# A short convolution's taps loaded in another way, beside newly chosen loads and schedule constants, in a fused convolution and gated-MLP kernel

## The chip, the cores and the metric

The kernel runs on one core of a Trainium2 chip. Its time is the device time of one execution in microseconds (us), and the median of several runs is what is compared. One further execution was recorded by the hardware profiler; its page and its trace are quoted below. The engines are PE (TensorE; PEld is its weight load), DVE (VectorE), ACT (ScalarE), POOL (GpSimd) and SP (SyncE, which here only issues DMA transfers). ACTq and SPq in a row are an engine's own queue issuing a DMA.

## The reference

The input x is 2048 x 640 in bf16. It is normalized, and the sum of x, a long convolution block (A) and a gated MLP (B) is returned.

```
xn = layernorm(x)
# A: a causal convolution of 4 taps over k, times v, then a convolution as long as the sequence
k_shift = sum over t of k_pad[:, t:t+S, :] * shift_k[:, 3-t]
kv = k_shift * v
y  = irfft(rfft(pad(kv)) * rfft(pad(ssm_k)))[:S] + kv * ssm_D
A  = xn * y
# B
h  = sigmoid(xn @ w_gate) * (xn @ w_up)        # 640 -> 1728
B  = h @ w_down                                # 1728 -> 640
return x + A + B
```

shift_k has the shape 640 x 4: for one channel its four taps lie side by side in memory.

## The kernel before

Rows of the sequence lie 16 to a partition (row 16 p + b in partition p), and the 640 channels are worked in five chunks c of 128. The MLP goes in four turns t of 512 rows. Within a turn, `gate(fc)` and `up(fc)` are each five matmuls of 128x512 for a block fc of 128 hidden columns (L246, L258). ScalarE puts the sigmoid of the gate into sig (L249), VectorE multiplies it with the up product into hT (L264). In some blocks ScalarE first casts the up product from PSUM (L261), and VectorE multiplies in place (L262). `both` does the last 64 columns, and `down` (L285) the product with wd, in two halves of seven matmuls for each 128 rows and 320 columns. The layernorm of a turn's rows is a chain on VectorE with the root on GpSimd (`ln_stats`, `ln_rstd`, `ln_nmr`, `ln_xn`), and `xn_tr` turns the result by TensorE into xnT (L217, copied at L220 or L222).

The long convolution is a Fourier transform in two stages for kv and for ssm_k side by side. `h_tr` turns ssm_k (tile hn) by TensorE into kvh (pht, L303). `kv_op` makes the four-tap convolution on VectorE: 16 operations of 128x1024 per chunk (L318 to L327), which read kx and the taps sc, laid out as tap by channel and the same in every partition. `st1` is the first stage (ps, L345), written to DRAM by `wr1` and read back in another order by `rd2` (tile t). `st2` (L373), `prod` (DVE) and `inv1` (L403) follow, then `wr2` and `rdb` go through DRAM again (tile bi), and `inv2` (psb, L435) ends a quarter of a chunk.

The taps are brought in through DRAM. At the start ScalarE's queue issues `tapT.rearrange("m d -> d m") <- A_shift_k` (L445), which turns 640 x 4 into 4 x 640, in single elements of two bytes. `load_taps(c)` (L143, on SyncE's queue) then reads four rows of 128 of it, broadcast to all partitions, into one of two buffers sc.

The start is written out by hand: four loads of x, the turned taps, weights in column blocks of 256 (`load_w`: a gate load and an up load each), then taps, kx and v of chunk 0 on SyncE, and dcl (ssm_D) and hn of chunk 0 on ScalarE's queue. TensorE runs 15 idle matmuls, then transposes of four row blocks with three idle matmuls between, then the first two blocks fc in half products of 256 columns (`half`, L236). `add_D` (POOL, L296) adds ssm_D to hn, and `h_tr(0)` follows.

All that follows is put in order when the program is built, by a planner that is itself in the kernel. It keeps for every engine when it is free and for every result when it is ready, by costs in the code, and emits the step that it holds to be ready. Each engine then works through its instructions in that order and waits where the plan was too early. A DMA costs the planner 0.45 on SP, at least 1.4 to start, its duration, and 1.6 until its data count as landed. DUE, slack, TURN and TH steer which chain comes first: DUE the step from which layernorm goes ahead of the tap products on VectorE, slack how far ahead of time a group of loads may be issued, TURN how the two ends of the convolution chain alternate on TensorE, and TH from which backlog of VectorE an up product is cast by ScalarE first. The transfers share eight completion semaphores in turn, so that an issue waits until the transfer eight before it has landed.

Of the kernel before, what the change touches and what calls it, by code (L numbers as in the profile page):

```python
# [10 lines left out]
BF16 = mybir.dt.bfloat16  # L11
F32 = mybir.dt.float32
U16 = mybir.dt.uint16
ACT = mybir.ActivationFunctionType
# [3 lines left out]
DM = 640  # L18
FF = 1728
P = 128  # L20
NB = S // P
NC = DM // P
NFC = 14
# [11 lines left out]
def _tables():  # L35

    p = np.arange(P)  # L40
    k1 = p + 0.25
    s1 = np.zeros((P, NB, 2, P))
    for b in range(NB):
        psi = 2 * np.pi * k1[None, :] * (16 * p + b)[:, None] / 2048.0
        s1[:, b, 0, :] = np.cos(psi)
        s1[:, b, 1, :] = -np.sin(psi)
    tb = s1.transpose(3, 2, 1, 0) / 2048.0
    th = 2 * np.pi * np.outer(np.arange(NB), np.arange(NB)) / 16.0
    c, s = np.cos(th), np.sin(th)
    s2 = np.block([[c, -s], [s, c]])  # L50
    a1 = np.block([[c.T, s.T], [-c.T, -s.T]])
    a2 = np.block([[-s.T, c.T], [-s.T, c.T]])
    small = np.stack([s2, a1, a2], 1)
    return _bf16_bits(s1), _bf16_bits(tb), _bf16_bits(np.concatenate([small] * NQ, 0))
# [3 lines left out]
def kernel(  # L58
# [14 lines left out]
    nc = tc.nc  # L73
# [6 lines left out]
    Dcol = A_ssm_D.rearrange("(d o) -> d o", o=1)  # L80

    s1bits, tbbits, smbits = _tables()
    S1d = nc.inline_tensor(s1bits, name="tabS1")
    TBd = nc.inline_tensor(tbbits, name="tabTB")
    SMd = nc.inline_tensor(smbits, name="tabSM")
# [2 lines left out]
    cv = ctx.enter_context(tc.tile_pool(name="cv", bufs=1))  # L88
    dr = ctx.enter_context(tc.tile_pool(name="dr", bufs=1, space=bass.MemoryType.DRAM))
# [30 lines left out]
    sync = nc.sync  # L120
    ctx.enter_context(tc.manual_schedule())

    tapT = dr.tile([4, DM], BF16, name="tapT")


    cin = [dict() for _ in range(NC)]

# [4 lines left out]
    def load_h(c, eng, n, lo, hi):  # L132
        d = cin[c]
        if n == 0:
            d["hn"] = cv.tile([P, S], BF16, name="hn")
            d["dcl"] = cv.tile([P, 1], BF16, name="dcl")
            eng.dma_start(d["dcl"][:, :], Dcol[c * P:(c + 1) * P, :])  # L137
        eng.dma_start(d["hn"][:, lo:hi], A_ssm_k[c * P:(c + 1) * P, lo:hi])

    def load_taps(c):  # L140
        sc = cv.tile([P, 4, P], BF16, name="sc", bufs=2)
        src = tapT.rearrange("(o m) d -> o m d", o=1)[:, :, c * P:(c + 1) * P]
        sync.dma_start(sc[:, :, :], src.to_broadcast((P, 4, P)))  # L143
        cin[c]["sc"] = sc

    def load_k(c, lo, hi):
# [13 lines left out]
    def load_w(eng, lo, hi):  # L160
        eng.dma_start(w[:, :, lo:hi], wgr[:, :, lo:hi])
        h = min(hi, 13 * P)
        eng.dma_start(w[:, :, UP + lo:UP + h], wur[:, :, lo:h])
        if hi == FF:
            eng.dma_start(w[:, :, FF:UP], wur[:, :, h:FF])
# [276 lines left out]

    for i in range(4):
        (sync, nc.scalar)[i % 2].dma_start(x[:, i, :], xr[:, i, :])
    nc.scalar.dma_start(tapT.rearrange("m d -> d m"), A_shift_k)  # L445
    load_w(sync, 0, 256)
    load_h(0, nc.scalar, 0, 0, S)
    load_w(sync, 256, 512)
    load_taps(0)
    load_halo(0)  # L450
    load_k(0, 0, NB)
    load_w(sync, 512, 768)
# [50 lines left out]
    def opsready(ops):  # L503
        made = set(m for o in ops for m in o[3])
        return max(when([t for t in o[2] if t not in made]) for o in ops)

    def emit(step):
        fn, args, ops = step
        ops = ops()
        fn(*args)  # L510
        for eng, dur, need, make in ops:
            at = when(need)
            if eng == "DMA":
                free["SP"] = max(free["SP"], at) + 0.45
                free["DMA"] = max(free["DMA"], free["SP"] + 1.4) + dur
                end = free["DMA"] + 1.6
            else:
                free[eng] = max(free[eng], at) + dur
                end = free[eng] + LAG[eng]
            for m in make:  # L520
                ready[m] = end
                if m[0] in count:
                    count[m[0]] += 1
# [12 lines left out]
    def prior(tag, *k):  # L536
        return (tag,) + k if min(k) >= 0 else None
# [77 lines left out]
    def s_load(fn, args, occ, need, make):  # L615
        return fn, args, lambda: [("DMA", occ, need, make)]

    chains = dict(sp=[], dve1=[], ln=[], kv=[], pool=[], inv=[], mid=[], front=[], out=[], sp_b=[], sp_k=[],
                  sp_v=[], sp_t=[], sp_h=[], bulk=[], sp_w1=[], sp_w2=[])
    for c in range(NC):  # L620
        if c:
            last = [prior("kvn", c - 2, 13)]
            chains["sp_t"].append(s_load(load_taps, (c,), 0.4, [prior("kvn", c - 2, 14)], [("taps", c)]))
            back = [("htr", c - 1, 1)] if c > 1 else []
            chains["sp_h"] += [s_load(load_h, (c, sync, 0, 0, 1024), 0.7, back, []),
                               s_load(load_h, (c, sync, 1, 1024, 2048), 0.7, back, [("hn", c)])]
            chains["sp_k"].append(s_load(load_halo, (c,), 0.3, last, [("hal", c)]))
            for i in range(4):
                chains["sp_k"].append(s_load(load_k, (c, 4 * i, 4 * i + 4), 0.7, last, [("k", c)] if i == 3 else []))
            for i in range(4):  # L630
                chains["sp_v"].append(s_load(load_v, (c, 4 * i, 4 * i + 4), 0.7, [prior("st1", c - 2, 7)],
                                             [("v", c)] if i == 3 else [("va", c)]))
            chains["pool"].append((add_D, (c,), lambda c=c: [("POOL", 0.35, [("hn", c)], [("D", c)])]))
        chains["front"] += [s_htr(c, 0), s_htr(c, 1)]
        chains["kv"] += [s_kv(c, [8 * h + n for n in ns]) for h in range(2)
                         for ns in ((0,), (1, 2), (3, 4), (5, 6), (7,))]
        chains["front"] += [s_st1(c, n) for n in range(8)]
        chains["sp_w1"] += [s_wr1(c, i) for i in range(4)]
        for s in range(4 * c, 4 * c + 4):
            chains["sp"].append(s_rd2(s))  # L640
            chains["mid"].append(s_st2(s))
            chains["dve1"] += [s_prod(s, 0), s_prod(s, 1)]
            if s % 2:
                chains["inv"].append(s_inv1(s // 2))
                chains["sp_w2"].append(s_load(wr2, (s // 2,), 2.4, [("ao", s // 2)], [("d2", s // 2)]))
        chains["sp_b"] += [s_rdb(c, n) for n in range(2)]
        chains["last"] = chains.get("last", []) + [s_inv2(c, m) for m in range(4)]
    def s_w(lo, hi):
        return load_w, (sync, lo, hi), lambda: [("DMA", (hi - lo) * 0.0095, [], [("w", f) for f in range(lo // P, NFC)])]

    def s_wd(lo, hi):
        return s_load(load_wd, (sync, lo, hi), 0.5 * (hi - lo), [], ["wd"] if hi == NFC else [])

    def s_x(g):
        return s_load(load_x, (sync, g), 1.8, [], [("x", g)])
# [2 lines left out]
    bulk.append((sync.dma_start, (SMt[:], SMd.ap()), lambda: [("DMA", 0.2, [], ["SM"])]))  # L658
    bulk.append(s_w(768, 1024))
    bulk.append((sync.dma_start, (S1t[:], S1d.ap()), lambda: [("DMA", 2.9, [], ["S1"])]))  # L660
    bulk += [s_w(1024, 1280), s_w(1280, FF), s_wd(0, 7), s_wd(7, NFC), s_x(1)] + chains["sp_v"][:4]
    bulk += chains["sp_h"][:2] + chains["sp_k"][:5]
    del chains["sp_k"][:5], chains["sp_v"][:4], chains["sp_h"][:2]
    chains["bulk2"] = bulk = [s_x(2), s_x(3)]
    bulk.append((sync.dma_start, (TBt[:], TBd.ap()), lambda: [("DMA", 2.9, [], ["TB"])]))
# [73 lines left out]
        emit(chains[k][pos[k]])  # L739
        pos[k] += 1  # L740

    DUE = (18, 20, 24)
    slack = dict(bulk=5.0, sp_k=3.0, sp_v=3.0, sp_h=2.0, bulk2=1.5)

    def side(now, at):

        again = True
        while again:
            again = False
            for k in ("sp_w1", "sp", "sp_w2", "sp_b", "sp_t", "bulk", "sp_k", "sp_v", "sp_h", "bulk2", "out"):  # L750
                h = head(k)
                if k in slack and free["DMA"] > now + slack[k]:
                    continue
                if h and free["SP"] < now + 0.5 and opsready(h[2]()) <= now + 0.1:
                    issue(k)
                    again = True
                    break
            for k in ("pool",):
                h = head(k)
                if h and free["POOL"] < now + 0.5 and opsready(h[2]()) <= now + 0.2:  # L760
                    issue(k)
                    again = True
            due = at >= DUE[min(pos["ln"] // 10, 2)]
            for k in ("dve1",) + (("ln", "kv") if due else ("kv", "ln")):
                h = head(k)
                if h and free["DVE"] < now + 1.2 and opsready(h[2]()) <= max(now, free["DVE"]) + 0.1:
                    issue(k)
                    again = True
                    break

    at, credit, TURN, TH = 0, 0, 2, 0.5
    while at < len(seq) or any(head(k) for k in chains):
        now = free["PE"]
        side(now, at)
# [55 lines left out]
```

## Time and profile before

| | before |
|---|---|
| median of 3 runs | 260.72 us (260.69 to 261.73) |
| the profiled execution | 261.89 us |
| its span | 260.1 us |
| TensorE busy | 244.8 us (94%) |
| VectorE busy | 182.3 us (70%) |
| ScalarE busy | 155.7 us (60%) |
| GpSimd busy | 9.0 us (3%) |
| moved by DMA | 54.85 MB |

A row of the timeline has the start, the duration, engine, line, operation, the tile written and the tile read, a count, and in brackets the idle time before it and what ended it. A row of the chain has the start, the length, and what the end of the kernel hung on in that time. A row of the stretches has, for a window in us, its length, the busy time of PE, PEld, DVE, ACT and POOL with their instruction counts, the granted TensorE clock, the share of the DMA engines in use, and GB/s. A row of the DMA issues ends with KB per transfer and the median us from issue to landing. A row of the groups has the shapes, a count, busy us and mean ns of one, and idle time before them.

### The profile page before, as it was taken

How to read it: one execution, taken by the hardware profiler on the slowest of the kernel's cores; microseconds unless marked ns; L12 is line 12 of the kernel's file. 1: busy time of each engine (PE TensorE's matmuls, PEld its weight loads, DVE VectorE, ACT ScalarE, POOL GpSimd, SP SyncE). 2: the span in 40 equal slices, each digit the busy share in tenths (PEclk: the TensorE clock that was granted, in tenths of full speed). 3: DMA queues.
4: the chain of work that ended last, by engine and by line, in shares of the span. 5: the costliest groups of instructions: out<-in, count | busy, mean ns of one | idle time of the engine just before them, and what ended most of it. 6: DMA issues, size and time to landing. Idle time of an engine off the chain costs nothing.

```text
span 260.1 us, 5955 instructions
## 1 busy us (share of the span) xinstructions
PE 244.8 (94%) x2469; PEld 143.7 (55%) x2469; DVE 182.3 (70%) x346; ACT 155.7 (60%) x198; POOL 9.0 (3%) x23
## 2 busy tenths in 40 slices
PE   8096899999999999999999999999999999999994
PEld 2054444557764545546786564555677554545773
DVE  4312069638799999999989998896617766873263
ACT  2141336653349788875587876998679667665000
POOL 4200000000100020010000000000000000000000
PEclk9659599999999999999999999999999999999999
DMA  7993799999999899985473999637569668481613
GB/s 169 48 76 90 173 231 357 336 349 304 255 255 335 214 323 318 262 228 174 130 203 131 245 321 334 206 107 229 179 211 257 152 179 216 147 285 47 192 48 122
DMA packets 92918, 54.85 MB, mean 211 GB/s; under 512 B 53532, under 2 KB 85980, under 8 KB 92636
## 3 DMA queue, kind: packets, MB, share of 16 engines
q1 hardware_dynamic: 89740, 53.62, 74.7%
q10 hardware_dynamic: 3152, 0.86, 3.0%
q8 instruction: 19, 0.31, 0.5%
q14 instruction: 7, 0.06, 0.1%
HBM read 36.12 MB, written 18.36 MB: 209 GB/s over the span
## 4 chain that ended last, share of the span: by engine, by line
PE 86%; DMA 10%; ACTq 3%; DVE 0%; issue 0%; POOL 0%; POOLq 0%
PE pd L285 24%; PE pu L258 21%; PE pg L246 20%; PE ps L345 7%; DMA hn<-in_A_ssm_k_dram 6%; PE psb L435 4%; PE psa L403 3%; PE ps L373 3%; ACTq L137 3%; DMA bi<-d 2%; PE pht L303 2%; PE pg L270 2%; PE pt L217 1%; DMA x<-in_A_q_dram 1%; DVE x L288 0%
## 5 line engine op out<-in xcount | busy, mean ns | idle before, releaser
L285 PE MATMUL pd<-wd,hT 128*128 128x320 bf16 x448 | 65.0, 299 | 0.0
L246 PE MATMUL pg<-xnT,w 128*128 128x512 bf16 x250 | 63.3, 385 | 0.0
L258 PE MATMUL pu<-xnT,w 128*128 128x512 bf16 x250 | 63.2, 384 | 0.0
L285 PEld LDWEIGHTS <-hT 128*128 128x128 bf16 x448 | 42.8, 98 | 17.5 <-issue 1.1
L249 ACT ACTIVATE sig<-pg 128x512 bf16<-128x512 f32 x52 | 31.5, 606 | 27.3 <-PE pg L246 23.9
L264 DVE TENSOR_TENSOR hT<-sig,pu 128x512 bf16<-128x512 bf16 x37 | 25.2, 681 | 28.3 <-PE pu L258 24.2
L376 ACT CAST xz<-ps 128x1024 bf16<-128x1024 f32 x40 | 38.5, 1018 | 9.0 <-PE ps L373 9.0
L348 ACT CAST t<-ps 128x1024 bf16<-128x1024 f32 x40 | 38.7, 1027 | 5.1 <-PE ps L345 4.0
L246 PEld LDWEIGHTS <-w 128*128 128x128 bf16 x250 | 23.9, 99 | 28.8 <-issue 2.4
L258 PEld LDWEIGHTS <-w 128*128 128x128 bf16 x250 | 23.8, 99 | 26.7 <-issue 2.7
L288 DVE TENSOR_TENSOR x<-pd,x 128x320 bf16<-128x320 f32 x32 | 15.5, 488 | 20.1 <-PE pd L285 19.8
L387 DVE TENSOR_TENSOR xz<-xz 128x2048 bf16<-128x2048 bf16 x20 | 24.5, 1224 | 0.6
L324 DVE TENSOR_TENSOR acc<-acc,tmp 128x1024 bf16<-128x1024 bf16 x30 | 20.8, 692 | 1.0
L345 PE MATMUL ps<-kvh,S1t 128*128 128x256 bf16 x160 | 20.9, 273 | 0.0
L322 DVE TENSOR_TENSOR tmp<-kx,sc 128x1024 bf16<-128x1024 bf16 x30 | 20.5, 685 | 0.2
L408 ACT CAST ao<-psa 128x1024 bf16<-128x1024 f32 x16 | 15.5, 1027 | 5.4 <-PE psa L403 5.4
L345 PEld LDWEIGHTS <-S1t 128*128 128x128 bf16 x160 | 15.6, 98 | 5.0
L186 DVE BATCH_NORM_STATS2 st<-x 128x6 f32<-128x320 bf16 x32 | 13.9, 477 | 2.6 <-DMA x<-in_A_q_dram 2.6
L304 ACT COPY kvh<-pht 128x1024 bf16<-128x1024 bf16 x10 | 9.7, 1036 | 9.8 <-PE pht L303 9.8
L439 DVE TENSOR_TENSOR yx<-psb,xn 128x512 bf16<-128x512 f32 x20 | 13.8, 689 | 1.3
L385 DVE STREAM_SHUFFLE xz<-xz 128x512 f32<-128x512 f32 x20 | 14.5, 727 | 0.1
L217 PE MATMUL pt<-ident,xn 128*128 128x128 bf16 x80 | 7.5, 237 | 6.5 <-ACT xn L203 6.5
(48 smaller groups left out, 173.2 us busy)
## 6 DMA issues: line engine op xcount, KB each, us to landing
d<-t SPq DMA_DIRECT2D x20, 512.0 KB, 4.7
t<-d SPq DMA_DIRECT2D x20, 512.0 KB, 5.4
d<-ao SPq DMA_DIRECT2D x8, 512.0 KB, 4.5
bi<-d SPq DMA_DIRECT2D x8, 512.0 KB, 5.3
kvh<-in_A_v_dram SPq DMA_DIRECT2D x16, 128.0 KB, 4.5
hn<-in_A_ssm_k_dram SPq DMA_DIRECT2D x8, 256.0 KB, 3.9
kx<-in_A_k_dram SPq DMA_DIRECT2D x16, 128.0 KB, 3.2
x<-in_A_q_dram SPq DMA_DIRECT2D x3, 640.0 KB, 6.2
```

The source lines that it names most:

```text
L246: nc.tensor.matmul(pg[:, :], lhsT=w[:, c, fc * P:(fc + 1) * P], rhs=xnT[:, c, :], start=(c == 0), stop=(c == NC - 1))
L249: nc.scalar.activation(sig[fc][:, :], pg[:, :], ACT.Sigmoid)
L258: nc.tensor.matmul(pu[:, :], lhsT=w[:, c, UP + fc * P:UP + (fc + 1) * P], rhs=xnT[:, c, :], start=(c == 0), stop=(c == NC - 1))
L264: nc.vector.tensor_tensor(hT[:, fc, :], sig[fc][:, :], pu[:, :], ALU.mult)
L285: nc.tensor.matmul(pd[:, :], lhsT=hT[:, fc, bb * P:(bb + 1) * P], rhs=wd[:, fc, es], start=(fc == 0), stop=(fc == NFC - 1))
L288: nc.vector.tensor_tensor(x[:, b, es], pd[:, :], x[:, b, es], ALU.add)
L322: nc.vector.tensor_tensor(d["tmp"][:, :, :], kx[:, lo + 3 - m:hi + 3 - m, :], sb(m), ALU.mult)
L324: nc.vector.tensor_tensor(d["acc"][:, :, :], d["acc"][:, :, :], d["tmp"][:, :, :], ALU.add)
L345: nc.tensor.matmul(ps[:, i, :], lhsT=S1[:, b, h, :], rhs=cin[c]["kvh"][:, b, :, :], start=True, stop=True)
L348: nc.scalar.copy(out=d["t1"][:, o:o + 4, :, :].rearrange("p b s c -> p b (s c)"), in_=ps[:, :, :])
L376: nc.scalar.copy(out=d["xz"][:, 0:2, 4 * n:4 * n + 4, :].rearrange("p s k c -> p k s c"), in_=ps[n].rearrange("p q e s c -> p (q e) s c"))
L387: nc.vector.tensor_tensor(xz[:, 1:3, :, :], xz[:, 0:1, :, :].to_broadcast((P, 2, 8, P)), xz[:, 1:3, :, :], ALU.mult)
```

## The change

The taps of a chunk, 128 x 4 numbers that lie together in memory, are now loaded as one run of 1 KB, the same for every partition (tile sraw), and an engine puts them into the order tap by channel (tile sc). GpSimd does so for chunk 0, ScalarE for the others. The turned copy in DRAM is gone. sc has one buffer in place of two, so the copy for a chunk follows the last tap product of the chunk before (`("kvn", c - 1, 14)`), and the load of sraw follows the copy of the chunk before. In the loads' order, the second row block of x (`s_x(1)`) goes ahead of the down weights, and chunk 1's hn and kx ahead of its v. The planner counts a DMA as landed after 1.2 in place of 1.6, and DUE, slack, TURN and TH have other values.

```diff
+    srow = A_shift_k.rearrange("d m -> (d m)").rearrange("(o n) -> o n", o=1)
...
-    tapT = dr.tile([4, DM], BF16, name="tapT")
...
     def load_taps(c):
-        sc = cv.tile([P, 4, P], BF16, name="sc", bufs=2)
-        src = tapT.rearrange("(o m) d -> o m d", o=1)[:, :, c * P:(c + 1) * P]
-        sync.dma_start(sc[:, :, :], src.to_broadcast((P, 4, P)))
+        cin[c]["sraw"] = cv.tile([P, 4 * P], BF16, name="sraw")
+        sync.dma_start(cin[c]["sraw"][:], srow[:, 4 * c * P:4 * (c + 1) * P].to_broadcast((P, 4 * P)))
+
+    def taps(c):
+        sc = cv.tile([P, 4, P], BF16, name="sc")
+        src = cin[c]["sraw"].rearrange("p (d m) -> p m d", m=4)
+        if c == 0:
+            nc.gpsimd.tensor_copy(sc[:, :, :], src)
+        else:
+            nc.scalar.copy(out=sc[:, :, :], in_=src)
         cin[c]["sc"] = sc
...
-    nc.scalar.dma_start(tapT.rearrange("m d -> d m"), A_shift_k)
     load_w(sync, 0, 256)
+    load_taps(0)
     load_h(0, nc.scalar, 0, 0, S)
     load_w(sync, 256, 512)
-    load_taps(0)
     load_halo(0)
...
-                end = free["DMA"] + 1.6
+                end = free["DMA"] + 1.2
...
-            chains["sp_t"].append(s_load(load_taps, (c,), 0.4, [prior("kvn", c - 2, 14)], [("taps", c)]))
+            chains["sp_t"].append(s_load(load_taps, (c,), 0.4, [("taps", c - 1)], [("sraw", c)]))
+            chains["act"].append((taps, (c,), lambda c=c: [("ACT", 0.6, [("sraw", c), ("kvn", c - 1, 14)],
+                                                            [("taps", c)])]))
...
-    bulk += [s_w(1024, 1280), s_w(1280, FF), s_wd(0, 7), s_wd(7, NFC), s_x(1)] + chains["sp_v"][:4]
-    bulk += chains["sp_h"][:2] + chains["sp_k"][:5]
+    bulk += [s_w(1024, 1280), s_w(1280, FF), s_x(1), s_wd(0, 7), s_wd(7, NFC)] + chains["sp_h"][:2]
+    bulk += chains["sp_k"][:5] + chains["sp_v"][:4]
...
-    DUE = (18, 20, 24)
-    slack = dict(bulk=5.0, sp_k=3.0, sp_v=3.0, sp_h=2.0, bulk2=1.5)
+    DUE = (8, 52, 56)
+    slack = dict(bulk=3.0, sp_k=3.0, sp_v=3.0, sp_h=1.5, bulk2=1.5)
...
-            for k in ("pool",):
+            for k, e in (("pool", "POOL"), ("act", "ACT")):
                 h = head(k)
-                if h and free["POOL"] < now + 0.5 and opsready(h[2]()) <= now + 0.2:
+                if h and free[e] < now + 0.5 and opsready(h[2]()) <= now + 0.2:
...
-    at, credit, TURN, TH = 0, 0, 2, 0.5
+    taps(0)
+    at, credit, TURN, TH = 0, 0, 4, 1.5
```

Since the order comes from the planner, the change moves rows on every engine. Three places follow. A row has the line, the operation, and the tile written and read with its shape.

The first is the start of ScalarE's program, its queue's DMAs among it. Before:

```order
L444 DMA x<-in_A_q_dram 128x640
L118 ACT_TABLE_LOAD
L118 ACTIVATE warm<-mhalf 128x4
L444 DMA x<-in_A_q_dram 128x640
L445 DMA tapT<-in_A_shift_k_dram 640x4x1
L137 DMA dcl<-in_A_ssm_D_dram 128x1
L138 DMA hn<-in_A_ssm_k_dram 128x2048
L203 ACTIVATE xn<-x,nmr,rstd 128x640 x2
```

With the change:

```order
L450 DMA x<-in_A_q_dram 128x640
L119 ACT_TABLE_LOAD
L119 ACTIVATE warm<-mhalf 128x4
L450 DMA x<-in_A_q_dram 128x640
L136 DMA dcl<-in_A_ssm_D_dram 128x1
L137 DMA hn<-in_A_ssm_k_dram 128x2048
L209 ACTIVATE xn<-x,nmr,rstd 128x640 x2
```

The turned load of 640x4 single elements is gone from between x and dcl; the rest is the same.

The second is SyncE's program behind its loads of x: weights, taps, kx and its three rows of overlap, and the third weight block. Before:

```order
L161 DMA w<-in_B_w_gate_dram 128x5x256
L163 DMA w<-in_B_w_up_dram 128x5x256
L161 DMA w<-in_B_w_gate_dram 128x5x256
L163 DMA w<-in_B_w_up_dram 128x5x256
L143 DMA sc<-tapT 128x4x128
L151 DMA kx_85<-in_A_k_dram 112x3x128
L152 DMA kx_85<-in_A_k_dram 15x3x128
L147 DMA kx_85<-in_A_k_dram 128x16x128
```

With the change:

```order
L167 DMA w<-in_B_w_gate_dram 128x5x256
L169 DMA w<-in_B_w_up_dram 128x5x256
L141 DMA sraw<-in_A_shift_k_dram 128x512
L167 DMA w<-in_B_w_gate_dram 128x5x256
L169 DMA w<-in_B_w_up_dram 128x5x256
L157 DMA kx_85<-in_A_k_dram 112x3x128
L158 DMA kx_85<-in_A_k_dram 15x3x128
L153 DMA kx_85<-in_A_k_dram 128x16x128
```

The load of the taps no longer follows the turned copy, and stands one weight block earlier.

The third is SyncE's program around the down weights wd; d is the write of the first Fourier stage, t the tile it comes from. Before:

```order
L165 DMA w<-in_B_w_up_dram 128x5x64
L169 DMA wd<-in_B_w_down_dram 128x7x640
L354 DMA d_396<-t_397 128x2048
L169 DMA wd<-in_B_w_down_dram 128x6x640
L171 DMA wd<-in_B_w_down_dram 64x640
L143 DMA sc<-tapT 128x4x128
L130 DMA x<-in_A_q_dram 128x2560
```

With the change:

```order
L171 DMA w<-in_B_w_up_dram 128x5x64
L129 DMA x<-in_A_q_dram 128x2560
L360 DMA d_391<-t_392 128x2048
L175 DMA wd<-in_B_w_down_dram 128x7x640
L141 DMA sraw<-in_A_shift_k_dram 128x512
L175 DMA wd<-in_B_w_down_dram 128x6x640
L177 DMA wd<-in_B_w_down_dram 64x640
```

Both down-weight loads now stand behind the first write d, and the load of chunk 2's taps, which follows ScalarE's copy of chunk 1's, stands between them. That copy comes on ScalarE behind the sigmoid of the tenth block fc of the first turn.

More of the change, by code (lines that the diff above doesn't have):

```diff
@@ L616, in s_load @@
         return fn, args, lambda: [("DMA", occ, need, make)]
-    chains = dict(sp=[], dve1=[], ln=[], kv=[], pool=[], inv=[], mid=[], front=[], out=[], sp_b=[], sp_k=[],
+    chains = dict(sp=[], dve1=[], ln=[], kv=[], pool=[], act=[], inv=[], mid=[], front=[], out=[], sp_b=[], sp_k=[],
                   sp_v=[], sp_t=[], sp_h=[], bulk=[], sp_w1=[], sp_w2=[])
```

## The prediction

> **What bounds the kernel now.** I read the table of busy time by stretch first, then the chain of work that ended last, then the timeline of the first 30 us. The stretches (columns: length, PE, PEld, DVE, ACT and POOL busy with instruction counts, granted clock, DMA share, GB/s):
>
> ```profile
> 3.00:6.00 3.00, 3.00 (x10) 1.04 (x9) 2.21 (x7) 0.00 (x0) 0.60 (x2) 1.00 1.07 254
> 6.00:9.00 3.00, 0.76 (x4) 0.14 (x2) 2.71 (x13) 0.00 (x0) 1.22 (x3) 1.00 1.47 62
> 9.00:12.00 3.00, 0.00 (x0) 0.00 (x0) 0.00 (x0) 0.00 (x0) 0.44 (x1) 0.50 1.51 48
> ...
> 15.00:18.00 3.00, 3.00 (x16) 1.86 (x15) 1.00 (x3) 0.48 (x1) 0.00 (x0) 0.50 1.02 77
> ...
> 30.00:40.00 10.00, 10.00 (x40) 4.12 (x39) 4.99 (x8) 3.44 (x7) 0.00 (x0) 0.85 1.00 236
> 40.00:60.00 20.00, 20.00 (x110) 10.64 (x109) 12.08 (x21) 12.22 (x18) 0.00 (x0) 1.00 1.08 345
> ...
> 80.00:100.00 20.00, 20.00 (x195) 10.07 (x193) 19.55 (x40) 17.09 (x22) 1.51 (x2) 1.00 1.00 294
> ...
> 220.00:240.00 20.00, 20.00 (x253) 10.15 (x252) 13.64 (x23) 13.10 (x19) 0.00 (x0) 1.00 0.52 161
> ```
>
> From 30 us to 240 us TensorE is busy all the time (first and last of the ten stretches of 20 us are shown; the lowest has 19.71). So nothing behind the start can be shortened except TensorE's own work, which the change leaves alone. The start is another matter: before 27 us the DMA engines are more than full (shares 1.51 and 1.02) while they move 48 to 77 GB/s, a third of what they move at the same share elsewhere. The chain and the timeline say who does that:
>
> ```profile
> 3.88 6.76 ACTq L137
> 10.68 16.04 DMA hn<-in_A_ssm_k_dram
> 27.10 1.93 PE pht L303 x16
> 29.03 2.13 PE pg L246 x5
> 31.16 2.00 PE pu L258 x5
> 33.17 1.08 PE pg L246 x5
> ```
>
> ```profile
> 12.24 0.92 ACT L203 ACTIVATE xn<-x,nmr,rstd 128x640 bf16<-128x640 bf16 x1 [9.58 <-issue]
> 18.95 1.39 PE L236 MATMUL pg<-xnT,w 128*128 128x256 bf16 x10 [0.33 <-DMA w<-in_B_w_up_dram]
> 20.46 3.11 PE L236 MATMUL pg<-xnT,w 128*128 128x256 bf16 x25
> 25.21 0.37 SPq L143 DMA_DIRECT2D sc<-tapT  x1
> ```
>
> ```profile
> hn<-in_A_ssm_k_dram ACTq DMA_DIRECT2D x1, 512.0 KB, 16.0
> kx<-in_A_k_dram SPq DMA_DIRECT2D x1, 512.0 KB, 6.0
> tapT<-in_A_shift_k_dram ACTq DMA_DIRECT2D x1, 5.0 KB, 23.5
> ```
>
> The turned load of the taps moves 5 KB in 2560 single elements and lands after 23.5 us. Three things hang on it. ScalarE's queue is stuck in the issue behind it (6.76 us at L137), so ScalarE normalizes nothing before 12.24. hn, on the same queue, takes 16.0 us where 512 KB of kx take 6.0, and TensorE's pht at 27.10 waits for it. And SyncE's queue stands at the load of sc until 25.21, with kx, the third weight block and v behind it.
>
> The Trainium skill ("DMA: Bandwidth & Descriptors", Queues, rings and completion order) says that each DMA engine takes turns, packet by packet, between the queues that have work for it. The trace agrees: SyncE's weights crawl beside ScalarE's elements.
>
> **The change, part by part.** Milestone: the first full gate matmul (third weight column block), at 29.03 now. What lies behind it is 260.1 - 29.03 = 231.1 us, of which the first two matmul groups ran at half clock, 2.13 + 2.00 against 2 x 1.08: 1.97 us too many.
>
> When does that milestone come in the changed kernel? The first statistics are not touched:
>
> ```profile
> 6.14 0.15 DVE L196 SCALAR_TENSOR_TENSOR nmr<-mv,rstd 128x1 f32<-128x1 f32 x1
> 7.44 0.15 DVE L196 SCALAR_TENSOR_TENSOR nmr<-mv,rstd 128x1 f32<-128x1 f32 x1
> 13.22 0.71 PE L217 MATMUL pt<-ident,xn 128*128 128x128 bf16 x5 [6.46 <-ACT xn L203]
> 20.18 0.44 PE L217 MATMUL pt<-ident,xn 128*128 128x128 bf16 x5
> 13.97 0.69 ACT L220 COPY xnT<-pt 128x640 bf16<-128x640 bf16 x1
> ```
>
> With its queue free, ScalarE can start xn at 6.3 and end at 7.2; the first transposes stand at 7.3 in place of 13.22. The second xn waits for its statistics (7.6) and ends at 8.5, the third follows after a 0.69 copy and ends at 10.1. TensorE goes 7.3 + 0.44, three idle matmuls, transposes from 8.6 to 9.05, three idle matmuls (0.65 at full clock, by the 1.08 of five), and starts the half gates at 9.7. The 40 matmuls of these halves cost 3.11 / 25 = 0.124 each, 5.0 us, and two more transposes 0.88: done at 15.6. The weights have to be there at 9.7 and 10.9: x, two blocks of 320 KB and hn are 1.82 MB, at the 254 GB/s of 3 to 6 us 7.2 us after 2: about 9.2. hn is there too, so pht runs at once, half of 1.93 at full clock. The milestone comes at **16.6**, and 29.03 - 16.6 = 12.4 us are gained, with the half-clock excess 14.4.
>
> This takes the clock as full. The trace shows the clock at 1.00 for 6 to 9 us and at half from 9 us, some 2.5 us after the idle matmuls ended at 6.76; now the pause is 0.6 us. If the clock is half all the same, the prologue goes at the old pace: 13.22 to 23.57 is 10.35 us, and pht 1.93, so the milestone would be 7.3 + 12.3 = 19.6, 3.0 us later.
>
> The Trainium skill ("TensorE: Matmul & The Clock Gate", Part 1: The HAM clock gate) puts both the fall after an idle window and the rise after sustained work at about 3.4 us. By it the clock stays up here, the same sum. The trace has a slower rise: cold from 27.10 to 33.
>
> **Copies.** Four 512-element copies on ScalarE and one on GpSimd are new. Nearest rows:
>
> ```profile
> L261 ACT CAST hT<-pu 128x512 bf16<-128x512 f32 x13 | 7.6, 587 | 4.3 <-PE pu L258 4.0
> L262 DVE TENSOR_TENSOR hT<-sig,hT 128x512 bf16<-128x512 bf16 x13 | 5.4, 418 | 2.7 <-ACT hT L261 2.5
> L264 DVE TENSOR_TENSOR hT<-sig,pu 128x512 bf16<-128x512 bf16 x37 | 25.2, 681 | 28.3 <-PE pu L258 24.2
> L115 POOL MEMSET wd<- 64x640 bf16 x1 | 0.6, 621 | 0.0
> ```
>
> ScalarE: 4 x 0.59 = 2.4 us on an engine that is busy 12.22 to 17.09 of 20 us in the rows above; at the same time 11 of the 13 casts of L261 disappear (6.5 us), whose products go back to VectorE at 681 in place of 418 ns: 2.9 us. Both lie beside TensorE's work and I cost them at nothing; VectorE's cover is thin at 80 to 100 us (19.55 of 20), and if it is gone they cost up to 2.9. The GpSimd copy has no row of its kind: no less than the 0.6 of a fill, say up to 2. It starts when hn and sraw are there (about 10) and its reader, the first VectorE product, also waits for kx, which is issued behind the first up weights (9.2, eight transfers before it) and takes 6.0: 15.2. So nothing, or up to 0.5.
>
> **Down weights.** The new SyncE order has sraw of chunk 2 between the two down-weight loads, and that load waits until ScalarE has read sraw of chunk 1, a copy that stands behind the tenth gate's sigmoid. From 16.6, fifteen groups of 1.08 and one pair of st1 groups (0.87) bring that gate to 33.7, its sigmoid to 34.3, the copy's end to 34.9, the issue of the second down-weight load to about 35.4 and of its tail to 36.1.
>
> ```profile
> 47.70 0.83 SPq L171 DMA_DIRECT2D wd<-in_B_w_down_dram  x1
> 58.57 1.90 PE pd L285 x14
> 60.48 0.87 PE ps L345 x8
> wd<-in_B_w_down_dram SPq DMA_DIRECT2D x1, 80.0 KB, 9.6
> ```
>
> With 9.6 us to landing they are there at 45.7. TensorE comes to the second half of the first down product, after 22 + 1 groups of 1.08, four pairs of st1 at 0.87 and one half of 0.95, at 16.6 + 24.8 + 3.5 + 0.95 = 45.9. Before, the margin was 59.5 - 57.3 = 2.2 us; now it is 0.2. I take 0.5 us of waiting, between 0 and 2.5.
>
> **Schedule constants.** The planner now counts on a landing 0.4 us earlier. Its sum for a read of t is 0.45 + 1.4 + 1.8 + 1.2 = 4.85 us, before 5.25.
>
> ```profile
> t<-d SPq DMA_DIRECT2D x20, 512.0 KB, 5.4
> bi<-d SPq DMA_DIRECT2D x8, 512.0 KB, 5.3
> PEld L435 <- DMA bi<-d: 0.8, 1, 0.8
> PEld L373 <- DMA t<-d: 0.4, 1, 0.4
> ```
>
> The trace has 5.4, so TensorE may stand up to 0.5 us at a read that is placed tight; now it waits 1.2 us for such reads in all. All 28 reads tight would be 28 x 0.4 = 11.2, but a wait also moves every later step away from its data. Between 0 (or 1.2 better, if the new order spares the old waits) and 11.2 I take 1.0, near the row of today.
>
> **The sum**, against the profiled execution (261.89 us, its span 260.1 plus 1.79 around it): 261.89 - 14.4 + 0.5 + 1.0 = 249.0. The median of the runs, 260.72, lies 1.17 below that execution, so the forecast is **247.8 us**.
>
> **Rivals.** (a) The loads become the bound of the first phase. Up to the first down product all weights (6.6 MB), x twice, hn, k, v, a table, three taps and two writes are 12.1 MB. At the 236 GB/s of 30 to 40 us this takes 2 + 51.3 = 53.3 us, 7.4 more than 45.9; at the 345 GB/s of 40 to 60 us 37, no wait. For it: kx and v in short rows, the slow mix. Against it: after the stall all of SyncE's work was issued anew from 25.21 on, and the 20 us behind show the faster pace with the same kinds of loads. It would give up to 255.2; chance 0.17, spread between.
>
> (b) The clock stays half in the prologue: 250.8; chance 0.08.
>
> (c) Slower: one buffer of taps. ScalarE's copy for the next chunk waits in ScalarE's order for VectorE's last tap product of this chunk, with sigmoids behind it, and TensorE has four accumulators before it stops. If VectorE, full from 80 us on, runs a half chunk late (eight products of 0.69, 5.5 us) at each of the four copies, 22 us are lost: 261.89 - 14.4 + 22 - 1.17 = 268. It decides from 3.6 us per copy, where the gain is used up. Against it: at 40 to 60 us VectorE is 12.08 of 20 busy, and the planner keeps the copy back until those products are due. Chance 0.04.
>
> (d) Nothing is freed: the tiny load of dcl, also two bytes a partition, stays on ScalarE's queue, and were it the blocker, all would remain: 260.7. But its later loads on SyncE's queue land in a median of 4.7 us:
>
> ```profile
> dcl<-in_A_ssm_D_dram SPq DMA_DIRECT2D x4, 0.2 KB, 4.7
> ```
>
> Chance 0.02.
>
> **How the numbers follow.** The forecast has 0.69. Low end: milestone at 15.6, no new wait and the old 1.2 gone gives 261.89 - 15.4 - 1.2 - 1.17 = 244.1; I take 244.3. High end: it takes in (b), the milestone with 2.5 for the down weights and 3 for tight reads (251.8), and most of (a): 255. Half a per cent, 1.3 us, is about what a measurement of this kernel can tell from no change. Faster by more than that: the forecast, (a) and (b), 0.94; within: (d) and a little of (c), 0.02; slower: the rest of (c), 0.04.
>
> **What would show it.** Right, if the first xn on ScalarE starts at 6.3, pht at about 15.6 and the clock is full from 6 us on; if hn lands within 8 us of its issue; if TensorE's idle time behind the milestone stays under 2 us. The down weights: a wait of TensorE for wd at about 46 us. (a) would show as waits for w between 20 and 40 us at DMA shares of 1. (c) would show as ScalarE idle before the copies with VectorE as what ended it. What would make the prediction wrong: many small waits for t and bi in the middle, from the shorter landing time.

## The result and the profile after

| | before | changed |
|---|---|---|
| median | 261.23 us (260.69 to 263.47, 4 runs) | 252.49 us (251.14 to 254.44, 4 runs) |
| the profiled execution, its span | 261.89, 260.1 us | 254.44, 252.3 us |
| TensorE busy | 244.8 us | 239.5 us |
| VectorE, ScalarE busy | 182.3, 155.7 us | 184.4, 152.3 us |

The ratio is 0.9656, its 95% interval 0.9567 to 0.9744: faster by 3.4%. The median before is 0.5 us above the one shown with the prediction, because a fourth run (263.47 us) has joined the three. The forecast was 247.8 us in a range of 244.3 to 255.0; the time lies 4.7 us above the forecast and inside the range. The profiled execution is the slowest of the four, so its waits are probably at the upper end.

The stretches of the changed kernel, with the columns of before (length; PE, PEld, DVE, ACT, POOL busy; granted clock, DMA share, GB/s):

```profile
3.00:6.00 3.00, 3.00 (x12) 1.00 (x10) 2.26 (x8) 0.00 (x0) 0.60 (x2) 1.00 0.82 243
6.00:9.00 3.00, 1.61 (x15) 0.88 (x15) 2.66 (x12) 2.38 (x4) 1.30 (x3) 1.00 0.72 222
9.00:12.00 3.00, 2.97 (x30) 2.30 (x29) 1.00 (x3) 1.55 (x3) 0.36 (x1) 1.00 1.04 320
12.00:15.00 3.00, 2.96 (x29) 2.44 (x28) 1.18 (x2) 1.16 (x2) 0.76 (x2) 1.00 0.98 178
15.00:18.00 3.00, 3.00 (x26) 1.82 (x25) 0.69 (x1) 2.46 (x4) 0.00 (x0) 1.00 0.95 252
...
30.00:40.00 10.00, 10.00 (x56) 5.29 (x55) 9.70 (x22) 7.67 (x11) 0.00 (x0) 1.00 1.06 341
40.00:60.00 20.00, 18.15 (x154) 12.62 (x153) 14.48 (x28) 6.88 (x10) 1.21 (x2) 1.00 0.97 283
...
100.00:120.00 20.00, 18.66 (x245) 11.99 (x244) 16.79 (x36) 13.42 (x17) 1.38 (x1) 1.00 1.02 285
120.00:140.00 20.00, 16.71 (x221) 9.90 (x220) 15.30 (x30) 12.18 (x16) 0.19 (x1) 1.00 0.54 155
```

Two things are to be seen. The start is mended: from 6 to 18 us the DMA engines move 178 to 320 GB/s where they moved 48 to 77, and the clock is full. But where TensorE had been busy for 20.00 of 20 us, it now stands for 1.85, 1.34 and 3.29 us in three stretches. Two of these before the change (the third, 40 to 60 us, stands in the prediction):

```profile
100.00:120.00 20.00, 20.00 (x236) 10.44 (x233) 19.20 (x42) 15.44 (x20) 1.20 (x2) 1.00 0.87 252
120.00:140.00 20.00, 20.00 (x320) 14.56 (x305) 18.50 (x34) 13.23 (x16) 0.00 (x0) 1.00 0.57 172
```

The timeline of the start, and the three large waits in the timeline of TensorE alone, all in the changed kernel:

```profile
6.25 0.92 ACT L209 ACTIVATE xn<-x,nmr,rstd 128x640 bf16<-128x640 bf16 x1 [3.59 <-DVE nmr L202]
9.64 0.71 PE L242 MATMUL pg<-xnT,w 128*128 128x256 bf16 x5
14.78 1.16 PE L309 MATMUL pht<-ident,hn 128*128 128x128 bf16 x16
15.78 1.24 PE L252 MATMUL pg<-xnT,w 128*128 128x512 bf16 x5
```

```profile
59.09 0.44 PE L379 MATMUL ps<-t,SMt 32*32 32x512 bf16 x16 [1.85 <-DMA t<-d]
108.80 0.31 PE L291 MATMUL pd<-wd,hT 128*128 128x320 bf16 x1 [1.25 <-DVE hT L280]
124.59 0.62 PE L441 MATMUL psb<-bi,TBt 128*128 128x128 bf16 x8 [2.73 <-DMA bi<-d]
```

The first xn starts at 6.25 (12.24 before). The milestone, the first full gate matmul, is at 15.94 in the chain of work; it was 29.03. That is 13.1 us, and with the 2.0 us of half clock 15.1 us are won. Some 7 us of it are given back later in this execution: from 16 to 240 us TensorE is busy 217.1 of 224 us.

### The profile page after: what moved, and what is told of

Read it like the earlier page. It is cut to its first block, busy times and chain, and to the rows that moved or that the text cites. A ratio compares the mean times of both kernels' runs of the same rounds, so it can differ in the third digit from the quotient of the medians.

```text
span 252.3 us, 5975 instructions
## 1 busy us (share of the span) xinstructions
PE 239.5 (95%) x2469; PEld 141.2 (56%) x2469; DVE 184.4 (73%) x346; ACT 152.3 (60%) x191; POOL 10.5 (4%) x24
## 4 chain that ended last, share of the span: by engine, by line
PE 75%; DMA 14%; ACT 5%; DVE 2%; issue 1%; SPq 1%; DVEq 0%
PE pg L252 20%; PE pu L264 19%; PE pd L291 16%; DMA bi<-d 8%; PE ps L351 6%; PE psb L441 4%; PE psa L409 3%; DMA d<-ao 3%; ACT xz L382 2%; PE ps L379 2%; DMA t<-d 2%; PE pg L242 2%; PE pht L309 1%; DMA x<-in_A_q_dram 1%; PE pt L223 1%
## 5 line engine op out<-in xcount | busy, mean ns | idle before, releaser
L291 PE MATMUL pd<-wd,hT 128*128 128x320 bf16 x448 | 65.0, 300 | 1.2 <-DVE hT L280 1.2
L252 PE MATMUL pg<-xnT,w 128*128 128x512 bf16 x250 | 62.2, 380 | 0.6 <-ACT xnT L226 0.6
L264 PE MATMUL pu<-xnT,w 128*128 128x512 bf16 x250 | 62.2, 380 | 0.0
L291 PEld LDWEIGHTS <-hT 128*128 128x128 bf16 x448 | 42.8, 98 | 19.3 <-DVE hT L280 1.6
L270 DVE TENSOR_TENSOR hT<-sig,pu 128x512 bf16<-128x512 bf16 x48 | 32.7, 681 | 25.3 <-PE pu L264 18.9
L382 ACT CAST xz<-ps 128x1024 bf16<-128x1024 f32 x40 | 38.6, 1022 | 16.6 <-PE ps L379 16.6
L226 ACT COPY xnT<-pt 128x640 bf16<-128x640 bf16 x14 | 9.6, 699 | 8.4 <-PE pt L223 8.2
L441 PEld LDWEIGHTS <-TBt 128*128 128x128 bf16 x160 | 9.5, 98 | 5.7 <-DMA bi<-d 3.7
```

The lines of the kernel that those rows point to most:

```text
L252: nc.tensor.matmul(pg[:, :], lhsT=w[:, c, fc * P:(fc + 1) * P], rhs=xnT[:, c, :], start=(c == 0), stop=(c == NC - 1))
L264: nc.tensor.matmul(pu[:, :], lhsT=w[:, c, UP + fc * P:UP + (fc + 1) * P], rhs=xnT[:, c, :], start=(c == 0), stop=(c == NC - 1))
L270: nc.vector.tensor_tensor(hT[:, fc, :], sig[fc][:, :], pu[:, :], ALU.mult)
L291: nc.tensor.matmul(pd[:, :], lhsT=hT[:, fc, bb * P:(bb + 1) * P], rhs=wd[:, fc, es], start=(fc == 0), stop=(fc == NFC - 1))
L382: nc.scalar.copy(out=d["xz"][:, 0:2, 4 * n:4 * n + 4, :].rearrange("p s k c -> p k s c"), in_=ps[n].rearrange("p q e s c -> p (q e) s c"))
L441: nc.tensor.matmul(ps[:, i, :], lhsT=TB[:, h, 4 * m + i, :], rhs=bi[:, h, 4 * (m % 2) + i, :], start=(h == 0), stop=(h == 1))
```

## The experiments

Each expectation was written before its run. Medians are from different sets of runs, so where a few us matter the ratio to the kernel before, with its 95% interval, is the safer number.

**The taps alone, the constants alone.** The first kernel is the changed one with all constants and the loads' order of before; the second is the kernel before with the new ones.

```diff
-                end = free["DMA"] + 1.2
+                end = free["DMA"] + 1.6
-    DUE = (8, 52, 56)
+    DUE = (18, 20, 24)
-    at, credit, TURN, TH = 0, 0, 4, 1.5
+    at, credit, TURN, TH = 0, 0, 2, 0.5
```

(slack and the order of the bulk loads likewise; the second kernel has the same lines the other way round.)

> The new way of the taps with the loads' order and all schedule constants of before. The profile of the changed kernel has its milestone (first full gate matmul) at 15.94 us, 13.1 earlier, and 2.0 less of half clock, but about 7 us of new waits of TensorE between 57 and 140 us. Theory P (the new constants place steps too early, and so make the waits): the waits go, 261.2 - 15.1 + 0.5 = 246.6 us, ratio to before 0.94. Theory R (the earlier start itself makes them: TensorE no longer trails the loads, and any order meets full DMA engines): waits of 6 us or more stay, 252 us or more, ratio 0.965 or more.

Measured: 252.75 us, ratio 0.9709 (0.9638 to 0.978). This is what R expected, but for another reason. The milestone is at 16.0 here too; only 2.8 us are lost in the middle. The rest is lost at the end, as VectorE's timeline of this kernel shows:

```profile
242.46 0.49 DVE L294 TENSOR_TENSOR x<-pd,x 128x320 bf16<-128x320 f32 x1 [1.41 <-PE pd L291]
243.57 0.69 DVE L445 TENSOR_TENSOR yx<-psb,xn 128x512 bf16<-128x512 f32 x1 [0.62 <-PE psb L441]
...
248.06 0.42 DVE L446 TENSOR_TENSOR x<-x,yx 128x512 bf16<-128x512 bf16 x1
```

The last down product is added at 242.9, and the last four products of the convolution follow alone until 248.5. In the order before, 42 down matmuls stood behind them; here none do. A new step in the planner (the copy) made another order, and this one puts the convolution last.

> The taps as before, through the turned copy, with the new order of loads and the new constants. Theory P: the new waits come in here too, 261 + 5 to 7 = 266 to 268 us. Theory R: the start is as late as before, so the new constants meet the same room as the old: 261 us, within 2.

Measured: 263.59 us, ratio 1.0107 (1.0039 to 1.0175). Between the two theories: the new constants cost under the late start, too, but 1% and not 2%.

**Single constants of the changed kernel.** In the first the landing time goes back to 1.6, in the second TURN and TH go back to 2 and 0.5, in the third the landing time is 2.0.

> The changed kernel with one constant back: a transfer counts as landed after 1.6 us in place of 1.2. If the landing time is what makes the waits (the part of P that the prediction priced at 1.0 us): 247 to 248 us and TensorE's waits for t and bi under 2 us in all. If not: 251 to 253 us.

Measured: 249.67 us, 0.9591 (0.9509 to 0.9672), the fastest of these, and TensorE's waits for bi are 2.4 us with none for t. It points to the landing time, but its interval and that of the change overlap.

> The changed kernel with TURN and TH of before (2 and 0.5). If the alternation or the fewer casts on ScalarE make the waits: 247 to 249 us. If they serve the earlier start (R): 252 us or more, with more casts at the line of the up product and ScalarE busier.

Measured: 257.47 us, 0.9872 (0.9808 to 0.9935), 5 us slower than the change. As in e1_taps_alone, the last products of the convolution come behind the last down product, on VectorE from 246.2 to 251.1 us. So in these kernels, with the copy in the plan, the new TURN and TH bring the convolution forward; with the old ones it ends last.

> The changed kernel with a landing time of 2.0 us in the planner (changed: 1.2, 252.5 us; 1.6: 249.7 us). If TensorE's waits come from steps placed ahead of their data, they shrink further and the time is 247 to 249 us. If the convolution chain, placed later, now ends behind the MLP, as with the old TURN and TH: 250 us or more, with an idle TensorE in the last 10 us.

Measured: 250.55 us, 0.9587 (0.9522 to 0.9652). Not further down than at 1.6: a later landing alone doesn't bring the waits to nothing.

**Does TensorE lack lead?** The changed kernel with a later TensorE:

```diff
-    busy(15)
+    busy(73)
```

> The changed kernel with 73 idle matmuls in place of 15 ahead of the first transposes, so that TensorE starts its work some 12 us later (58 x 0.216 = 12.5), while the loads and the order of everything stay. If the waits behind the start come from too little lead of loads and of the other engines over TensorE, they go for the greater part, and the time is 252.5 + 12.5 - 5 to 7 = 258 to 260 us. If the order itself makes them, whatever the lead: 264 to 266 us.

Measured: 263.0 us (260.95 to 265.76, 10 runs), 1.0075 (1.0027 to 1.0123). The first half gate moved from 9.64 to 20.58, by 10.9 us, and the median rose by 10.5: by the medians nearly the whole shift stays. The profiles are less clear. TensorE's waits for bi and t (us in total, times, longest), first in the changed kernel, then in this one:

```profile
PE psb L441 <- DMA bi<-d: 3.1, 3, 2.7
PE ps L379 <- DMA t<-d: 1.9, 1, 1.9
```

```profile
PE ps L379 <- DMA t<-d: 0.4, 1, 0.4
PE psb L441 <- DMA bi<-d: 0.4, 1, 0.4
```

These waits have nearly gone here, those for hT at L280 (1.2 us) and for xnT (0.6 us) are the same, and the span, 258.8 us, is only 6.5 above that of the changed kernel. But this execution is the fastest of its ten and that of the changed kernel the slowest of its four, so the pair can't tell what the lead does from what differs between executions. The medians speak against theory R of the first run; the kernel with the order of before, further down, decides.

**Where the copies run.** All five on GpSimd:

```diff
-        if c == 0:
-            nc.gpsimd.tensor_copy(sc[:, :, :], src)
-        else:
-            nc.scalar.copy(out=sc[:, :, :], in_=src)
+        nc.gpsimd.tensor_copy(sc[:, :, :], src)
...
```

(The planner's step of the copy likewise counts on GpSimd, 0.7 us in place of ScalarE's 0.6.)

> The changed kernel with all five copies of the taps on GpSimd (row of the changed profile: 0.64 us for one). ScalarE is relieved of 4 x 0.67 = 2.7 us. By the prediction they lie beside other work and cost nothing: 252.5 us within 1. If they stand in a full stretch of ScalarE (at 97 us one does, ahead of the casts behind which the last sigmoid of the second turn came late): 251 us or less.

Measured: 251.25 us, 0.9634 (0.9559 to 0.9708). Not told apart from the change; the planner's order is another one here as well, and a single wait for t has 3.0 us. Behind it the granted clock is 0.57 from 60 to 64 us, and 14 down matmuls take 3.66 us in place of 2.06.

**Two buffers of taps**, with the landing time of 1.6. A buffer st of the layernorm makes room:

```diff
-        sc = cv.tile([P, 4, P], BF16, name="sc")
+        sc = cv.tile([P, 4, P], BF16, name="sc", bufs=2)
-            chains["act"].append((taps, (c,), lambda c=c: [("ACT", 0.6, [("sraw", c), ("kvn", c - 1, 14)],
+            chains["act"].append((taps, (c,), lambda c=c: [("ACT", 0.6, [("sraw", c), prior("kvn", c - 2, 14)],
```

> The changed kernel with a landing time of 1.6 us (e3_land16, 249.7 us) and two buffers sc, the copy waiting for the chunk before last. If the single buffer costs something: 247 to 248.5 us. If not, 249.7 us within 1, since the planner makes yet another order.

Measured: 250.66 us, 0.9644 (0.9584 to 0.9704): no gain over one buffer (249.67 us), though the planner makes yet another order. Nothing here shows the prediction's slower rival, ScalarE held up by the single buffer.

**The half clock.** The changed kernel with one idle matmul at the start and none between the transposes:

```diff
-    busy(15)
+    busy(1)
...
-            busy(3)
```

> The changed kernel without its idle matmuls (1 in place of 15, and none between the first transposes). By the prediction's rival of the half clock, the prologue then goes at half clock, with the milestone at 19 to 19.6 in place of 15.94: 3 to 3.6 us later, so 255.5 to 256 us if all of it stays. If TensorE only waits less behind it, as the theory of too little lead has it: 253 to 254 us. If the clock rises all the same at once: 252.5 us.

Measured: 254.06 us, 0.9734 (0.9656 to 0.9811). The milestone is at 18.2, 2.3 us later, not 3 to 3.6:

```profile
9.97 1.23 PE pg L242 x5
11.73 2.13 PE pg L242 x10
14.27 0.55 PE pg L242 x5
14.85 2.36 PE pg L242 x20
17.21 1.00 PE pht L309 x16
```

In this chain ten half-gate matmuls take 2.13 us at first, and twenty take 2.36 from 14.85 on: the clock rises within the prologue. The median is 1.6 us higher, though the two intervals overlap.

**The order of before, kept.** If the order is the cause, the new taps must be tried under the old order. Here the planner sees `load_taps` as before, and the copy is issued on GpSimd beside it, into two buffers. TensorE, VectorE, ScalarE and SyncE then have the program of before, row for row, but for the turned load that is gone and sraw in sc's place. Here, too, st has one buffer to make room.

```diff
+    def taps(c):
+        sc = cv.tile([P, 4, P], BF16, name="sc", bufs=2)
+        nc.gpsimd.tensor_copy(sc[:, :, :], cin[c]["sraw"].rearrange("p (d m) -> p m d", m=4))
+        cin[c]["sc"] = sc
...
     def kv_op(c, n):
+        if n == 8 and c + 1 < NC:
+            taps(c + 1)
```

> The new way of the taps under the order of before: TensorE, VectorE, ScalarE and SyncE have row for row the program of before (without the turned load; sraw stands where sc stood); the copies go to GpSimd, into two buffers sc, so that the planner needs no new step. Theory O (the waits of the changed kernel and the late end of the taps alone come from the newly made orders): all of the start's 15.1 us stay, 261.2 - 15.1 + 0 to 1.5 = 246 to 247.6 us, ratio 0.943 to 0.948. Theory L (that order met its data in time only because TensorE trailed the loads by 13 us): waits of 4 us or more appear, 250 us or more, ratio above 0.957.

Measured: **246.51 us** (246.23 to 246.61), ratio 0.9471 (0.9429 to 0.9514). Theory O holds, and R falls with L, for the start is as early as in the changed kernel (milestone at 15.91): the interval lies below that of the change, and the runs are 0.4 us apart where those of the change were 3.3. The sums of the stretches from 16 to 240 us, of the change and of this kernel:

```profile
sum 224.00, PE 217.10 PEld 126.71 DVE 172.45 ACT 145.20 POOL 5.04; mean PE 24.12 PEld 14.08 DVE 19.16 ACT 16.13 POOL 0.56
```

```profile
sum 224.00, PE 221.82 PEld 131.90 DVE 173.69 ACT 148.35 POOL 6.61; mean PE 24.65 PEld 14.66 DVE 19.30 ACT 16.48 POOL 0.73
```

TensorE is idle 2.2 us in place of 6.9 (and 23 matmul records are missing from this trace, so rather less). VectorE and ScalarE are a little busier in the same time, and TensorE's longest wait for any engine or transfer behind the milestone is 0.3 us. The order of before had been made for a TensorE free at 14.3 us (`free = dict(PE=14.3, ...)`), and only now does TensorE come near it.

> The kernel of e9_order_before with 73 idle matmuls in place of 15, which moved the first half gate 10.9 us later in e5_late_pe. Theory O: nothing waits for loads, so the whole shift stays: 10.9 us above e9_order_before, 257 to 258.5 us. Theory L: the waits go with the shift, and it lies 4 to 7 us above e9_order_before, 256 to 258 us with that one at 250 or more; the difference between the two tells.

Measured: 258.36 us, 0.9941 (0.9912 to 0.997), 11.9 us above e9_order_before. The first half gate moved from 9.62 to 21.39, by 11.8 us and not by 10.9, so the whole shift stays, where theory L had 4 to 7 us. The old order doesn't need the late TensorE either.

**The new constants without the new step.** As the last, the kernel of e9_order_before with the new constants and loads' order; TensorE has the rows of e2_consts_alone.

> The kernel of e9_order_before (246.5 us) with the new order of loads and the new constants; the planner still knows no step for the copies, so TensorE has row for row the order of e2_consts_alone. If the constants make the waits of the changed kernel: 250 us or more. If they are made only by the constants together with the new step of the taps in the plan: 246 to 248 us. From e2_consts_alone, 2.8 us above the kernel before with the same order, 249.3 us is to be expected.

Measured: 248.94 us (248.3 to 249.21), 0.9546 (0.9482 to 0.961), as worked out from e2_consts_alone. TensorE is busy 221.0 of 224 us from 16 to 240, 3.0 idle (22 matmul records are missing here, so rather less):

```profile
sum 224.00, PE 221.01 PEld 131.07 DVE 176.88 ACT 142.85 POOL 8.17; mean PE 24.56 PEld 14.56 DVE 19.65 ACT 15.87 POOL 0.91
```

So the steps are: new taps under the old order 246.5, with the new constants 248.9 (2.4 more; 0.75% by the ratios), with the copy as a step of the plan on ScalarE and one buffer 252.5 (3.6 more; 1.1% by the ratios). For both steps the intervals of the ratios overlap, while the single runs of the kernels compared don't. The copy as a step under the old constants has 252.75, 6.2 more than without it. What in the step makes the worse order isn't settled: under the new constants, GpSimd in ScalarE's place and two buffers in place of one each changed the time by less than the runs can tell. Both together, as in e9_order_before, weren't tried with the step in the plan.

## Why the prediction was right, and where it was off

**What bounds the kernel** was read rightly: TensorE, behind a start held up by the turned load. Without that load hn lands 9.3 us after its issue, where it took 16.0 (the prediction's own test had asked for 8), and no weight is late.

**The start** was worked out at 14.4 us with a milestone at 16.6. It came to 15.1 and 15.94; the half gates began at 9.64, forecast 9.7. The prologue at full clock held. The pause behind the idle matmuls was 1.2 us, not 0.6, and left the clock full. Before the change the clock fell at 9.0 us, 2.2 us after the idle matmuls' end at 6.76, and not the 2.5 that the prediction read. The Trainium skill ("TensorE: Matmul & The Clock Gate", Part 1: The HAM clock gate) puts the fall after an idle window of about 3.4 us. The short pause here agrees with it; the fall before came sooner, and there the measurement decides.

**Copies** at nothing. Their groups in the changed kernel, busy us and mean ns behind the shapes:

```profile
L149 ACT COPY sc<-sraw 128x512 bf16<-128x512 bf16 x4 | 2.7, 663 | 0.0
L147 POOL COPY sc<-sraw 128x512 bf16<-128x512 bf16 x1 | 0.6, 636 | 0.0
```

The size was nearly right (0.59 and 0.6 to 2 had been taken), and no run ties a wait to the copies themselves. That the copy as a step of the planner makes another order wasn't seen at all.

**Down weights**, 0.5 us: no wait. TensorE goes from the first half of the down product through st1 to the second half without a gap at 43 to 45 us. The last of the weights landed at 44.5, 0.6 us before the second half at 45.05; the prediction had 0.2 between them. The true cost is 0, inside the bounds that were given.

**Schedule constants**, taken at 1.0 between 0 and 11.2: this is the term that was mis-sized. The whole cost of the new order is 6.0 us (252.49 against 246.51; 4.8 by the ratios), of which 2.4 belong to the constants and 3.6 to the new step. The prediction priced only reads that are placed 0.4 us too early. The largest wait is one of that kind, and it is much longer than 0.4 us: psb at 124.59 waits 2.73 us for a read of bi issued at 115.98 that took the longest of its kind, 8.6 us. With the old landing time of 1.6, TensorE still waited 2.4 us for bi (e3_land16). The issue and the times to landing (min, median, max) of bi in the changed kernel, and the second row in e9_order_before:

```profile
115.98 0.81 SPq L431 DMA_DIRECT2D bi<-d  x1
DMA to landing us min/median/max: 3.9/5.7/8.6
```

```profile
DMA to landing us min/median/max: 4.0/5.2/7.2
```

The wait at L291 isn't for a transfer at all: the chain of the changed kernel before 109 us runs over ScalarE's casts (t, xz) and copies (kvh) to the last sigmoid of the turn.

```profile
101.82 1.92 ACT t L354 x2
103.74 1.02 ACT kvh L310 x2
104.76 0.66 issue
105.42 1.99 ACT xz L382 x2
107.43 0.60 ACT sig L279
108.05 0.70 DVE hT L280
```

Three pairs of them stand ahead of the sigmoid L279, and the down product waits for it. The order on ScalarE's queue made this wait; under the order of before there is none, and the prediction looked at no place of that kind.

Of the prediction's signs of being right, three came (the first xn, pht and the clock) and two failed: hn took 9.3 us and not 8, and TensorE's idle time behind the milestone was 6.9 us and not under 2. Its sign of being wrong, waits for t and bi in the middle, came too, as a few long ones and not as many small ones. That the time still lies inside the range is in part luck: the upper end of 255 us counted 3 us for tight reads, and held 6.0 only because it was also made for a half clock, late down weights and slow loads, none of which came.

**Rivals.** (a), loads as the bound of the first phase, is out: TensorE is busy throughout from 18 to 40 us at DMA shares of about 1. (b) didn't come, the clock stayed full; without the idle matmuls the milestone is 2.3 us later, where 3.0 had been priced. (c) doesn't show: no idle time of ScalarE lies ahead of the copies (0.0 in their row), and neither two buffers nor GpSimd brought a gain that the runs can tell. (d) is out, since the first xn starts at 6.25.

## What to carry to other kernels

The transfer of single elements cost far more than its bytes: 5 KB held ScalarE's and SyncE's queues and crowded the DMA engines for up to 23 us, and broadcasts of 1 KB rows, one for each chunk with a copy of 0.65 us, replaced it. When a planner orders the program, measure a change under the order of before first, here by keeping the new work out of the plan; otherwise the gain of the change and the luck of a new order are read as one number. The best version found is the new taps under the order of before (e9_order_before), 246.5 us, faster than both kernels.

## What was not expected of the hardware

The granted clock of the profile reads 1.00 in the first stretches while the matmuls still run at half pace: in e8_cold it is 1.00 from 9 to 12 us, where five 256-column matmuls take 1.23 us and later 0.55 to 0.59. The pace of the rows, not that column, told when the clock rose.

```profile
9.00:12.00 3.00, 2.33 (x16) 1.65 (x15) 1.00 (x3) 1.16 (x3) 0.43 (x1) 1.00 1.14 334
```
